# Chunked RWKV attention and a two-matmul channel mix on one core: r, k, v loaded as fp32 on SyncE's queue, matmul pieces taken from a queue, centring on ScalarE and the inverse root on GpSimd

## The chip, the core and the metric

The program runs on one core of one Trainium2 chip. A core has five engines with a queue of instructions each, executed in order: TensorE (PE, with its weight loads listed apart as PEld), VectorE (DVE), ScalarE (ACT), GpSimd (POOL) and SyncE (SP). Engines wait for each other by semaphores. Transfers from and to the memory outside the core are issued by SP, ACT or POOL and run on 16 DMA engines. The metric is the time of one execution in microseconds (us) on the device.

## What is computed

The inputs r, k and v have the shape 4 x 8 x 768 x 48 (batch, heads, time, head size), w and u 8 x 48. The first half is a linear attention with a decaying state, the second a layer norm and a channel mix with a residual:

```python
for t in range(S):
    cur = u * kt outer vt
    y[t] = rt @ (state + cur)
    state = w * state + kt outer vt
x = y as (B, S, 384)
xn = (x - mean) / sqrt(var + 1e-6) * g_ln
out = x + max(xn @ w_ch1, 0) @ w_ch2        # 384 -> 1536 -> 384
```

## The kernel before

Time is cut into chunks of 128 steps, so there are 24 tiles (4 batches of 6 chunks), each with time on the 128 partitions and 8 x 48 = 384 columns. A setup computes the powers of w (tile `T`), transposes them to the factor tile `F2`, and builds `mask`, `WLZ` and `uwI`.

For tile i the attention half runs as four pieces of code:

- `scale(i)`: r and k, packed in `rk`, are multiplied by `F2` into one of three buffers `sc`, one VectorE instruction (line 180).
- `transposes(i)`: eight TensorE transposes of `sc` into the PSUM tile `tr` (line 188), copied to `trs` by ScalarE (line 190); VectorE multiplies the two halves to `q` (line 192).
- `scores(i)`: eight matmuls into `at` (line 203), and the state and the bonus term into `s` (lines 215, 225, 235). VectorE masks `at` into `A` (two instructions, line 246) and makes the next state `Z` (line 260); ScalarE copies the bonus `cc` (line 253), GpSimd makes `Vb` from it (line 255).
- `values(i)`: matmuls into `y` (lines 276, 288); VectorE adds `Vb` to give `x` (line 298), then the statistics `stats` and `mv` (lines 302, 306) and the centred `xn` (line 308). For every second tile ScalarE takes a square root and VectorE a reciprocal: `rs` (lines 314, 315).

The channel mix works on groups of two tiles (256 columns). `ln_transposes(i)` transposes `xn` (line 327, into the same PSUM tile `tr`; copy on ScalarE, line 328). `up(g, m)` is one of six pieces of a group: six matmuls of 256 columns into `hp` (line 337) and a ReLU on ScalarE into `hT` (line 344). `down(i, m)` is one of three pieces of a tile: four matmuls of 384 columns into `o` (line 355). There is one PSUM buffer for `o`. After the third piece VectorE scales it and adds `x` (`ot`, line 364), and SP stores `ot`. `g_ln` is folded into the weights `w1_sb` in the setup, by ScalarE (line 172).

The order on every engine is the order of the code. The loop at line 396 runs over steps s: attention of tile s, three up pieces of the group of tile s - 3, three down pieces of tile s - 5, placed by hand:

```python
        up_slot(s, 0); down_slot(s, 0)
        scores(s);     scale(s + 1)
        up_slot(s, 1); ln_transposes(s - 1)
        down_slot(s, 1); values(s)
        up_slot(s, 2); down_slot(s, 2)
```

with `transposes(s)` and the load of tile s + 3 ahead of it (the lines are shortened here). Loads of r, k and v are issued by GpSimd and change fp32 to bf16 on the way; a load reads 128 x 8 pieces of 192 bytes. They stand in GpSimd's queue behind `Vb` (line 255) of the step before.

## Time and profile before

| | |
|---|---|
| time, median of 3 runs | 182.71 us (181.68 to 182.91) |
| time of the profiled execution | 183.27 us |
| its span, first to last instruction | 181.2 us |
| PE busy | 148.7 us (82%), 1646 matmuls |
| DVE busy | 125.7 us (69%) |
| ACT busy | 87.3 us (48%) |
| POOL busy | 85.9 us (47%), with the issuing of its DMAs |

Busy time is the time in which an engine executes something; matmuls are pipelined, so that their start-to-start distance, and not their length, says how dense TensorE is. The span is cut into stages below, since the first quarter, the middle and the end have different limits. "Idle before" in brackets is the time in which the engine had nothing to do before an instruction, with what ended it. Queue q0 in the DMA views holds what GpSimd issues, q1 what SP and ACT issue.

### The profile page before, as it was taken

The page shows a single profiled execution, that of the slowest core. Times are in us where ns is not written, and L with a number is a line of the kernel's source. Part 1 is how long each engine was busy: PE and PEld are TensorE (multiplying, and loading weights), DVE is VectorE, ACT ScalarE, POOL GpSimd, SP SyncE. Part 2 cuts the span into 40 slices and gives each one's busy share as a digit, 9 for nine tenths or more (in the row PEclk, how much of TensorE's full clock was granted, in tenths as well). Part 3 has the DMA queues.
Part 4 walks back from the last instruction along what each step waited for, and adds up shares of the span by engine and source line. Part 5 has one row for each costly group of instructions (what it writes and reads, how often), then busy time and mean ns, then how long its engine had stood idle before and what let it go on. Part 6 is the DMA issues. An engine that isn't in the chain of part 4 may idle for free.

```text
span 181.2 us, 4089 instructions
## 1 busy us (share of the span) xinstructions
PE 148.7 (82%) x1646; PEld 110.1 (61%) x1646; DVE 125.7 (69%) x278; ACT 87.3 (48%) x162; POOL 85.9 (47%) x105
## 2 busy tenths in 40 slices
PE   0323558969998999999989999999899999989871
PEld 0212347757676677667666866776677767767640
DVE  0843989876798797878888877878797879621211
ACT  2085262465545453654546455637455555454300
POOL 7946776754773475357536733764471101100000
PEclk9999999988999999999999999999999999999999
DMA  5999999999889968998999799699967110111121
GB/s 21 244 340 141 184 175 79 63 67 65 43 83 97 96 48 79 109 52 84 89 109 56 75 89 111 37 87 99 93 51 77 47 45 0 47 43 45 43 90 43
DMA packets 81971, 15.61 MB, mean 86 GB/s; under 512 B 76960, under 2 KB 81568, under 8 KB 81952
## 3 DMA queue, kind: packets, MB, share of 16 engines
q0 software_dynamic: 76432, 8.26, 80.0%
q1 hardware_dynamic: 5520, 7.09, 11.2%
q8 instruction: 13, 0.21, 0.5%
q14 instruction: 6, 0.05, 0.1%
HBM read 18.88 MB, written 4.72 MB: 130 GB/s over the span
## 4 chain that ended last, share of the span: by engine, by line
PE 47%; DVE 33%; issue 8%; DMA 5%; ACT 4%; SPq 2%; DVEq 0%
PE o L355 20%; PE hp L337 11%; DVE ot L364 8%; DVE stats L302 7%; DVE x L298 7%; DMA w_f<-in_moe_w_ch_dram 5%; PE at L203 5%; DVE xn L308 3%; DVE A L246 3%; DVE mv L306 2%; DVE Z L260 2%; ACT trs L190 2%; PE y L288 2%; PE s L215 2%; PE tr L327 2%
## 5 line engine op out<-in xcount | busy, mean ns | idle before, releaser
L355 PE MATMUL o<-w_sb,hT 128*128 128x384 bf16 x288 | 57.8, 325 | 8.0 <-DVE ot L364 7.7
L337 PE MATMUL hp<-xT,w_sb 128*128 128x256 bf16 x432 | 60.5, 277 | 0.0
L344 ACT ACTIVATE hT<-hp 128x512 bf16<-128x512 f32 x72 | 42.8, 597 | 25.4 <-PE hp L337 25.4
L255 POOL TENSOR_TENSOR Vb<-vv,cc 128x384 bf16<-128x384 bf16 x24 | 19.8, 826 | 66.5 <-ACT cc L253 66.5
L337 PEld LDWEIGHTS <-w_sb 128*128 128x128 bf16 x432 | 38.8, 99 | 5.1
L355 PEld LDWEIGHTS <-hT 128*128 128x128 bf16 x288 | 27.2, 97 | 23.0 <-issue 12.2
L246 DVE TENSOR_TENSOR A<-at,mask 128x512 bf16<-128x512 f32 x48 | 30.9, 685 | 9.5 <-PE at L203 9.2
L190 ACT COPY trs<-tr 128x1024 bf16<-128x1024 bf16 x24 | 24.2, 1006 | 9.1 <-PE tr L188 9.1
L364 DVE SCALAR_TENSOR_TENSOR ot<-o,rs,x 128x384 f32<-128x384 f32 x24 | 14.4, 602 | 15.1 <-PE o L355 15.1
L71 POOL DMA_DIRECT2D rk<-in_k_dram x24 | 22.6, 944 | 0.8 <-POOLq L432 0.8
L72 POOL DMA_DIRECT2D rk<-in_r_dram x24 | 21.3, 889 | 3.0 <-DMA vv<-in_v_dram 3.0
L73 POOL DMA_DIRECT2D vv<-in_v_dram x24 | 21.8, 907 | 0.0
L192 DVE TENSOR_TENSOR q<-trs 128x512 bf16<-128x512 bf16 x24 | 10.2, 425 | 14.9 <-ACT trs L190 14.8
L188 PE MATMUL tr<-ident,sc 128*128 128x128 bf16 x192 | 16.5, 236 | 4.1 <-DVE sc L180 4.1
L188 PEld LDWEIGHTS <-sc 128*128 128x128 bf16 x192 | 13.8, 106 | 7.6 <-DVE sc L180 5.1
L203 PE MATMUL at<-trs 48*128 48x128 bf16 x192 | 10.2, 229 | 8.5 <-ACT trs L190 8.5
L298 DVE TENSOR_TENSOR x<-y,Vb 128x384 f32<-128x384 f32 x24 | 13.3, 554 | 5.1 <-PE y L288 5.1
L203 PEld LDWEIGHTS <-trs 48*128 48x128 bf16 x192 | 5.8, 98 | 15.9 <-ACT trs L190 13.1
L308 DVE TENSOR_SCALAR xn<-x,mv 128x384 bf16<-128x384 f32 x24 | 14.1, 586 | 0.9
L253 ACT COPY cc<-s 128x8 f32<-128x8 f32 x24 | 4.0, 166 | 21.9 <-PE s L235 21.9
L302 DVE BATCH_NORM_STATS2 stats<-x 128x6 f32<-128x384 f32 x24 | 13.5, 560 | 0.8
L180 DVE TENSOR_TENSOR sc<-rk,F 128x768 bf16<-128x768 bf16 x24 | 13.4, 558 | 0.0
(49 smaller groups left out, 127.5 us busy)
## 6 DMA issues: line engine op xcount, KB each, us to landing
out_dram<-ot SPq DMA_DIRECT2D x24, 192.0 KB, 2.6
rk<-in_k_dram POOLq DMA_DIRECT2D x24, 96.0 KB, 3.3
rk<-in_r_dram POOLq DMA_DIRECT2D x24, 96.0 KB, 4.0
vv<-in_v_dram POOLq DMA_DIRECT2D x24, 96.0 KB, 3.9
w_f<-in_moe_w_ch_dram SPq DMA_DIRECT2D x3, 768.0 KB, 7.5
w_sb<-in_moe_w_ch_dram POOLq DMA_DIRECT2D x1, 1152.0 KB, 10.0
w_p<-in_w_dram SPq DMA_DIRECT2D x2, 0.8 KB, 2.0
u_p<-in_u_dram SPq DMA_DIRECT2D x2, 0.8 KB, 3.1
```

Of the source, the lines that this page charges most:

```text
L71: nc.gpsimd.dma_start(out=rk[:, 1], in_=k[b, :, s0 : s0 + L, :].rearrange("h t d -> t h d"))
L73: nc.gpsimd.dma_start(out=vv[:], in_=v[b, :, s0 : s0 + L, :].rearrange("h t d -> t h d"))
L188: nc.tensor.transpose(out=tp[:, j, :], in_=sc[:, j, :], identity=ident[:])
L190: nc.scalar.copy(out=tr[:], in_=tp[:].rearrange("p (a q) t -> p a q t", a=2))
L203: nc.tensor.matmul(out=at[:, par, p, :], lhsT=tr[p0 : p0 + D, 1, p, :], rhs=tr[p0 : p0 + D, 0, p, :], start=True, stop=True,)
L246: nc.vector.tensor_tensor(out=A[:, par], in0=at[:, par], in1=mask[:].unsqueeze(1).to_broadcast([P, HP, P]), op=ALU.mult,)
L298: nc.vector.tensor_tensor(out=x[:], in0=y[:, :C], in1=cc_t[i][:].rearrange("p h d -> p (h d)"), op=ALU.add)
L302: nc.vector.bn_stats(out=stats[:], in_=x[:])
L337: nc.tensor.matmul(out=hp[:, f, :], lhsT=w1_sb[:, kc, fk * P : (fk + 1) * P], rhs=xT_t[g][:, kc, :], start=(kc == 0), stop=(kc == CK - 1),)
L344: nc.scalar.activation(out=hT_t[g][:, 2 * m : 2 * m + 2, :], in_=hp[:], func=ACT.Relu)
L355: nc.tensor.matmul(out=o[:, :C], lhsT=hT_t[g][:, fk, j * P : (j + 1) * P], rhs=w2_sb[:, fk, :], start=(fk == 0), stop=(fk == FK - 1),)
L364: nc.vector.scalar_tensor_tensor(out=ot[:], in0=o[:, :C], scalar=mv_t[g][:, j : j + 1], in1=x_t[i][:], op0=ALU.mult, op1=ALU.add,)
```

## The change

It has these parts:

- r, k and v are loaded as fp32, without a change of type, by SP (k of tile 0 by ACT). SP's queue holds the loads of tiles 0 and 1, then the weights `w1_f`, now in three pieces of 512 columns, then tiles 2 and 3, and in step s the load of tile s + 4. The small loads of w, u and g move to ACT's queue.
- `F2` is fp32. VectorE scales k alone, GpSimd scales r and makes a bf16 copy `vv` of v. `Vb` is fp32.
- The weights are scaled by -g in pieces in step 1, a third each on ScalarE, VectorE and GpSimd. The sign makes up for a centring that gives mean - x.
- Centring (`xn`) is a ScalarE instruction in the step after (`center`); the inverse root is an add and a power on GpSimd. There is no square root on ScalarE and no reciprocal.
- `transposes(s + 1)` stands in step s, between the second and third group of matmuls.
- Up and down pieces go to two queues when their inputs are in the program; `fill(2)`, three times in a step, takes two of them, up and down in turn. The first piece of a tile's down is not taken in the same `fill` as the last of the tile before. Downs may begin in step 4.
- The setup's chain `wl`, `uwI`, `WLZ` runs on GpSimd; `hT` has 5 buffers, `x` 14, the loads 7.

```diff
-        rk = ld.tile([P, 2, H, D], BF16, name="rk")
-        nc.gpsimd.dma_start(out=rk[:, 1], in_=k[b, :, s0 : s0 + L, :].rearrange("h t d -> t h d"))
-        nc.gpsimd.dma_start(out=rk[:, 0], ...)
-        nc.gpsimd.dma_start(out=vv[:], ...)
+        rk = ld.tile([P, 2, H, D], FP32, name="rk")
+        vf = ld.tile([P, H, D], FP32, name="vf")
+        (k_eng or nc.sync).dma_start(out=rk[:, 1], in_=k[b, :, s0 : s0 + L, :].rearrange("h t d -> t h d"))
+        nc.sync.dma_start(out=rk[:, 0], ...)
+        nc.sync.dma_start(out=vf[:], ...)
...
     def scale(i):
-        nc.vector.tensor_tensor(out=sc_bufs[i % NSC][:, :, :, :D], in0=rk_t[i][:], in1=F2[:], op=ALU.mult)
+        sc = sc_bufs[i % NSC]
+        nc.vector.tensor_tensor(out=sc[:, 1, :, :D], in0=rk_t[i][:, 1], in1=F2[:, 1], op=ALU.mult)
+        nc.gpsimd.tensor_tensor(out=sc[:, 0, :, :D], in0=rk_t[i][:, 0], in1=F2[:, 0], op=ALU.mult)
+        vv = ld.tile([P, H, D], BF16, name="vv")
+        nc.gpsimd.tensor_copy(out=vv[:], in_=vf_t[i][:])
...
+    def scale_w1(n):
+        nc.scalar.activation(out=w1_sb[:, n, 0], in_=w1_f[:, n, 0], func=ACT.Copy, scale=g_neg[:, 0:1])
+        nc.vector.tensor_scalar(out=w1_sb[:, n, 1], in0=w1_f[:, n, 1], scalar1=g_neg[:, 1:2], ...)
+        nc.gpsimd.tensor_scalar(out=w1_sb[:, n, 2], in0=w1_f[:, n, 2], scalar1=g_neg[:, 2:3], ...)
...
-        nc.vector.tensor_scalar(out=xn[:], in0=x[:], scalar1=mv[:, i % GT, 0:1], scalar2=None, op0=ALU.subtract)
-            nc.scalar.activation(out=rs[:], in_=mv[:, :, 1], func=ACT.Sqrt, bias=eps_t[:], scale=1.0)
-            nc.vector.reciprocal(out=rs[:], in_=rs[:])
+    def center(i):
+        nc.scalar.activation(out=xn[:], in_=x_t[i][:], func=ACT.Identity, bias=mv[:, j, 0:1], scale=-1.0)
+            nc.gpsimd.tensor_scalar(out=rs[:], in0=mv[:, :, 1], scalar1=1e-6, scalar2=1.0, ...)
+            nc.gpsimd.tensor_tensor(out=rs[:], in0=rs[:], in1=expo[:], op=ALU.pow)
...
+    def fill(n):
+        clock[0] += 1
+        for _ in range(n):
+            can_up = ups and ups[0][0] <= clock[0]
+            can_down = downs and downs[0][0] <= clock[0] and clock[0] >= down_from[0]
+            if can_down and downs[0][2] == 0 and last_o[0] >= clock[0]:
+                can_down = False
+            if can_up and (turn[0] == 0 or not can_down):
+                _, g, m = ups.pop(0)
+                up(g, m)
...
+    for s in range(NT):
+        if s + 1 < NT:
+            scale(s + 1)
+        scores(s)
+        if s >= 1:
+            center(s - 1)
+        if s == 1:
+            scale_w1(0)
+        if s + 4 < NT:
+            load(s + 4)
+        if s == W2_SLOT:
+            nc.gpsimd.dma_start(out=w2_sb[:], in_=w2_src)
+        fill(2)
+        if s + 1 < NT:
+            transposes(s + 1)
+        fill(2)
+        if s >= 1:
+            ln_transposes(s - 1)
+        values(s)
+        if s == 1:
+            scale_w1(1)
+            scale_w1(2)
+        fill(2)
```

Three places show what moves. The first is SP's queue from the start of the program, of the changed kernel (before it held the small loads, `w_f`, and then only the 24 stores):

```order
L77 DMA w_c<-in_w_dram 128x3x1
L72 DMA rk<-in_r_dram 128x8x48
L73 DMA vf<-in_v_dram 128x8x48
L71 DMA rk<-in_k_dram 128x8x48
L72 DMA rk<-in_r_dram 128x8x48
L73 DMA vf<-in_v_dram 128x8x48
L97 DMA w_f<-in_moe_w_ch_dram 128x3x512 x3
L71 DMA rk<-in_k_dram 128x8x48
```

The last row is the first load of tile 2: it stands behind five loads and all of the weights `w_f`.

The second is VectorE's queue in a step of the middle, from `x` of a tile to the next `x`; first before, then of the change:

```order
L298 TENSOR_TENSOR x<-y,Vb 128x384
L302 BN_STATS stats<-x 128x6
L306 BN_AGGR mv<-stats 128x2
L308 TENSOR_SCALAR xn<-x,mv 128x384
L364 SCALAR_TENSOR_TENSOR ot<-o,rs,x 128x384
L192 TENSOR_TENSOR q<-trs 128x512
L246 TENSOR_TENSOR A<-at,mask 128x512 x2
L260 TENSOR_TENSOR Z<-s,WLZ 128x384
L180 TENSOR_TENSOR sc_164<-rk,F_146 128x16x48
```

```order
L322 TENSOR_TENSOR x<-y,Vb 128x384
L326 BN_STATS stats<-x 128x6
L330 BN_AGGR mv<-stats 128x2
L405 SCALAR_TENSOR_TENSOR ot<-o,rs,x 128x384
L204 TENSOR_TENSOR sc_133<-rk,F_155 128x8x48
L270 TENSOR_TENSOR A<-at,mask 128x512 x2
L284 TENSOR_TENSOR Z<-s,WLZ 128x384
L218 TENSOR_TENSOR q<-trs 128x512
```

`xn` is gone from between `mv` and `ot`, `sc` of the next tile stands ahead of `A` instead of behind `Z`, and `q` is that of the next tile.

The third is GpSimd's queue in steps 0 and 1 of the change (before, each `Vb` was followed by three loads):

```order
L279 TENSOR_TENSOR Vb<-vf,cc 128x384
L205 TENSOR_TENSOR sc_137<-rk,F_155 128x8x48
L207 CAST vv<-vf 128x384
L279 TENSOR_TENSOR Vb<-vf,cc 128x384
L190 TENSOR_SCALAR w_sb<-w_f,g_neg 128x512
L463 DMA w_sb<-in_moe_w_ch_dram 128x12x384
L190 TENSOR_SCALAR w_sb<-w_f,g_neg 128x512 x2
```

The first `Vb` is that of tile 0, the second that of tile 1: between them stand two instructions on the data of tile 2.

## Rows read from the trace of the kernel before

**Rows 1.** The page's part 1: busy time of each engine.

```profile
PE 148.7 (82%) x1646; PEld 110.1 (61%) x1646; DVE 125.7 (69%) x278; ACT 87.3 (48%) x162; POOL 85.9 (47%) x105
```

**Rows 2.** Windows by stage: stretch, length, busy us per engine (instructions), PEclk, DMA share, GB/s.

```profile
0.00:15.34 15.34, 2.55 (x14) 1.91 (x14) 5.92 (x31) 6.71 (x5) 11.17 (x20) 1.00 1.27 195
15.34:48.77 33.43, 25.65 (x299) 20.00 (x300) 26.44 (x57) 15.91 (x32) 22.70 (x26) 0.95 1.47 100
48.77:159.13 110.36, 104.46 (x1224) 77.55 (x1223) 89.61 (x186) 58.73 (x118) 51.99 (x60) 1.00 0.86 73
159.13:177.31 18.18, 16.00 (x112) 10.61 (x110) 3.08 (x7) 6.00 (x11) 0.00 (x0) 1.00 0.16 55
177.31:181.20 3.89, 0.00 (x0) 0.00 (x0) 0.62 (x1) 0.00 (x0) 0.00 (x0) 1.00 0.14 51
```

**Rows 3.** The chain that ended last: start us, length us, what.

```profile
4.71 9.13 DMA w_f<-in_moe_w_ch_dram
13.86 1.57 ACT w_sb L172
15.44 0.91 ACT trs L190
...
48.77 0.52 DVE ot L364
```

**Rows 4.** Timeline of TensorE in one middle step: start us, length us, instruction, [idle before].

```profile
98.77 0.81 PE L355 MATMUL o<-w_sb,hT 128*128 128x384 bf16 x4 [0.35 <-DVE ot L364]
99.51 0.40 PE L203 MATMUL at<-trs 48*128 48x128 bf16 x8
...
102.13 0.81 PE L337 MATMUL hp<-xT,w_sb 128*128 128x256 bf16 x6
102.78 0.81 PE L355 MATMUL o<-w_sb,hT 128*128 128x384 bf16 x4
103.43 0.61 PE L188 MATMUL tr<-ident,sc 128*128 128x128 bf16 x8
103.88 0.82 PE L337 MATMUL hp<-xT,w_sb 128*128 128x256 bf16 x6
105.00 0.81 PE L355 MATMUL o<-w_sb,hT 128*128 128x384 bf16 x4 [0.30 <-DVE ot L364]
```

**Rows 5.** Who waited for whom: us in total, times, longest us.

```profile
PE o L355 <- DVE ot L364: 7.7, 19, 0.7
```

**Rows 6.** DMA queue q1 in the stretches 1.8:2.4, 3.7:6 and 9:12: packets, MB, share.

```profile
q1 hardware_dynamic: 357, 0.00, 30.1%
...
q1 hardware_dynamic: 819, 0.02, 36.6%
...
q1 hardware_dynamic: 206, 1.14, 97.8%
```

**Rows 7.** DMA queue q0 in the stretch 16:17: packets, MB, share.

```profile
q0 software_dynamic: 1490, 0.14, 267.2%
```

**Rows 8.** The page's DMA issues: KB each, us from issue to landing.

```profile
w_sb<-in_moe_w_ch_dram POOLq DMA_DIRECT2D x1, 1152.0 KB, 10.0
```

**Rows 9.** Instructions by line: busy us, mean ns of one, idle before.

```profile
L344 ACT ACTIVATE hT<-hp 128x512 bf16<-128x512 f32 x72 | 42.8, 597 | 25.4 <-PE hp L337 25.4
L255 POOL TENSOR_TENSOR Vb<-vv,cc 128x384 bf16<-128x384 bf16 x24 | 19.8, 826 | 66.5 <-ACT cc L253 66.5
L298 DVE TENSOR_TENSOR x<-y,Vb 128x384 f32<-128x384 f32 x24 | 13.3, 554 | 5.1 <-PE y L288 5.1
...
masks.py:197 POOL MEMSET ident_f<- 128x128 f32 x1 | 0.2, 243 | 0.0
```

**Rows 10.** The tiles' view of two VectorE instructions: duration ns, least, median, most.

```profile
L308 DVE TENSOR_SCALAR xn<-x,mv x24: 419/619/843, 20.6 to 158.7; 128x384 bf16<-128x384 f32 x24
L180 DVE TENSOR_TENSOR sc<-rk,F x24: 545/546/705, 10.6 to 150.8; 128x768 bf16<-128x768 bf16 x24
```

More of the change, by code (lines that the diff above doesn't have):

```diff
@@ L83 @@
         for par in range(2):
-            nc.sync.dma_start(
+            nc.scalar.dma_start(
                 out=dst[par * DP : par * DP + D, :],
@@ L114 @@
     )
-    load(1)
-    load(2)
-    eps_t = const.tile([P, 1], FP32, name="eps_t")
-    nc.vector.memset(eps_t[:], 1e-6)
+    ident = const.tile([P, P], BF16, name="ident")
+    nc.vector.tensor_copy(ident[:], ident_f[:])
+    expo = const.tile([P, GT], FP32, name="expo")
+    nc.vector.memset(expo[:], -0.5)
+    NSC = 3
+    sc_bufs = []
+    for i in range(NSC):
+        t_ = const.tile([P, 2, H, DP], BF16, name=f"sc{i}")
+        nc.vector.memset(t_[:, :, :, D:DP], 0.0)
+        sc_bufs.append(t_)
+    WLZ = const.tile([P, HP, E2], FP32, name="WLZ")
+    nc.vector.memset(WLZ[:], 0.0)
+    uwI = const.tile([P, HP, 2], BF16, name="uwI")
+    nc.vector.memset(uwI[:], 0.0)
     T = const.tile([P, 2 * CK, L + 1], FP32, name="T")
@@ L243, in scores @@
             first = False
+        if c < NCH - 1:
+            if c > 0:
+                nc.tensor.matmul(
+                    out=s_ps[:, : HP * E2],
+                    lhsT=ident[:],
+                    rhs=Z_t[i - 1][:].rearrange("p q e -> p (q e)"),
+                    start=False,
+                    stop=True,
+                    skip_group_check=True,
+                )
+            for p in range(HP):
+                nc.tensor.matmul(
+                    out=s_ps[:, p * E2 : (p + 1) * E2],
+                    lhsT=ksc[:, 1, p, :],
+                    rhs=v_t[i][:, 2 * p : 2 * p + 2, :],
+                    start=False,
+                    stop=True,
+                    skip_group_check=True,
+                )
         A = sb2.tile([P, 2, HP, P], BF16, name="A")
@@ L253, in scores @@
         nc.scalar.copy(out=cc[:], in_=s_ps[:, C : C + H])
-        Vb = sb2.tile([P, H, D], BF16, name="Vb")
+        Vb = sb2.tile([P, H, D], FP32, name="Vb")
         nc.gpsimd.tensor_tensor(
-            out=Vb[:], in0=v_t[i][:], in1=cc[:].unsqueeze(2).to_broadcast([P, H, D]), op=ALU.mult
+            out=Vb[:], in0=vf_t[i][:], in1=cc[:].unsqueeze(2).to_broadcast([P, H, D]), op=ALU.mult
         )
@@ L328, in ln_transposes @@
         nc.scalar.copy(out=xT_t[g][:, :, j * P : (j + 1) * P], in_=tp[:, :CK, :])
+        if j == GT - 1:
+            for m in range(NU):
+                ups.append((clock[0] + 1, g, m))
+    NU = FK // 2
+    FB = FW // P
     def up(g, m):
         if m == 0:
-            hT_t[g] = sb2.tile([P, FK, GW], BF16, name="hT")
+            hT_t[g] = sb3.tile([P, FK, GW], BF16, name="hT", bufs=5)
         hp = ps_h.tile([P, 2, GW], FP32, name="hp")
         for f in range(2):
-            fk = 2 * m + f
+            n, fb = divmod(2 * m + f, FB)
             for kc in range(CK):
@@ L344, in up @@
         nc.scalar.activation(out=hT_t[g][:, 2 * m : 2 * m + 2, :], in_=hp[:], func=ACT.Relu)
+        if m == NU - 1:
+            for j in range(GT):
+                for d in range(NM):
+                    downs.append((clock[0] + 1, g * GT + j, d))
     NM = 3
@@ L373, in down @@
             nc.sync.dma_start(out=out[b, c * L : (c + 1) * L, :], in_=ot[:])
[L376 to L417 removed]
+    clock = [0]
@@ new lines @@
+    turn = [0]
+    last_o = [-9]
+    down_from = [99]
+    ups, downs = [], []
+    def fill(n):
[8 more added lines that the diff above has]
+                up(g, m)
+                turn[0] = 1
+            elif can_down:
+                _, i, d = downs.pop(0)
+                down(i, d)
+                if d == NM - 1:
+                    last_o[0] = clock[0]
+                turn[0] = 0
+            else:
+                break
@@ L421 @@
+    center(NT - 1)
+    fill(2)
+    ln_transposes(NT - 1)
+    while ups or downs:
+        fill(2)
 _INS = ['r', 'k', 'v', 'w', 'u', 'moe_g_ln', 'moe_w_ch1', 'moe_w_ch2']
```

195 lines of the change are left out of this document (79 added, 116 removed).

## The prediction

> **What bounds the kernel now.** I read busy time first: TensorE is busy for 82% of the span, the others for 69% or less [rows 1]. An average hides the stages, so the windows come next [rows 2]. Three limits show. Up to 15.34 us TensorE has 2.55 us of work: the chain of waits runs there through the third weight load (landing at 13.84) and the scaling of the weights on ScalarE, and only behind these, at 15.4, comes the first copy `trs` of the attention [rows 3]. From there to 48.77, where tile 0's `ot` runs, attention is latency-bound and the channel mix fills up slowly. From 48.77 to 159.13 there are 18 steps of 110.36 / 18 = 6.13 us, and TensorE is nearly full. The end is a tail of channel-mix pieces.
>
> The middle decides most. In a step's timeline [rows 4] an up piece lasts 0.65 us from start to start (102.13 to 102.78), a down piece 0.65 (102.78 to 103.43). The up piece at 103.88 is followed by the next down only at 105.00: 1.12 - 0.65 = 0.47 us lost, and the down then takes 0.74 instead of 0.65 to the next matmul (98.77 to 99.51), another 0.09. The list of waits says why: the single `o` buffer is held until `ot` has run, 19 times in 24 tiles [rows 5]. `ot` itself is late because `x`, `stats`, `mv` and `xn` stand ahead of it on VectorE. Without the wait the step is 105.00 - 98.77 - 0.56 = 5.67 us. First and last chunks of a batch leave out matmuls; by the start-to-start distances this is 0.7 us in six steps, so a dense step is 5.56 us on average.
>
> **The change, part by part.** *Middle.* The queue never puts a tile's first down into the same `fill` as the last of the tile before. By the program order at least a transposition and an up piece (0.45 + 0.65) lie between them, and `xn` is gone from VectorE, so `ot` should be done. Gain: (6.13 - 5.56) x 18 = 10.3 us. In the tail 18.18 us hold 8 up and 15 down pieces and a transposition, 15.1 us dense; the last two waits remain, as nothing is left to put between (about 0.75 us each), so 1.5 is gained.
>
> *New waits on TensorE.* `ln_transposes(s - 1)` now comes two pieces after `transposes(s + 1)`, and both use the one PSUM tile `tr`, so it waits for `trs`. Two pieces and the transposition are 1.75 us, the copy about 1.0 us plus its start; it just fits if ScalarE is free, and is late by up to one ReLU of 0.6 us [rows 9] if not. Bounds 0 and 0.6 a step; I take 0.1, 2 us in all, since one ReLU per `fill` mostly ends before the transposition does.
>
> *Load on the other engines, per step of 5.56.* VectorE has 89.61 / 18 = 4.98 us [rows 2]; it loses `xn` (0.6, [rows 10]); `sc` of half the columns from fp32 costs about what `x` with as many columns costs, 0.55 [rows 9], as before. That leaves 4.4. ScalarE has 58.73 / 18 = 3.3 and gets `xn`, at most a ReLU's 0.6: 3.9. GpSimd loses its DMA issues and has `r` (as `Vb`, 0.83), the copy of v (between the 0.24 of a memset and 0.83; taken 0.45), `Vb` 0.83 and, every second step, the add and the power. No row shows a power; between 0.1 and 0.83 each by the nearest rows, it is hidden by some 3 us of idle GpSimd either way. All this is cost at nothing while TensorE covers it.
>
> *Start.* Attention no longer waits for the weights. But the loads go to q1. No run shows 192-byte pieces there; the nearest row is that of the 4-byte pieces of the small loads: 357 packets in 0.6 us, 595 per us [rows 6], while GpSimd's queue moves 1,490 per us [rows 7]. At 595 a load of 1,024 pieces takes 1.72 us. Ahead of tile 2 stand 384 pieces of `w_c`, six loads of 1,024 and 1,152 small ones (7,680, or 12.9 us from 1.8 to 14.7), then 2.36 MB of weights at 1.14 MB in 3 us [rows 6], 6.2 us, to 20.9. Tile 2's k, r and v land at 22.6, 24.4 and 26.1, tile 3's v at 31.2, tile 4's at 36.4; tile 5's k at 38.1. `vv` of tile 2 is ahead of tile 1's `Vb` on GpSimd, so step 1 ends behind 26.1, step 2 behind 31.2, step 3 behind 36.4. After that come `vv` 0.45, `Vb` 0.83, `x` to `mv` 1.3 (39.0), `sc` 0.55 and `A` 1.3 of step 4 (40.9) and `y`: TensorE is through step 4's first two fills at about 42. At 48.77 the kernel before has done one attention step (5.67 - 3.9 = 1.8) and four up pieces (2.6) more, so the point that answers to 48.77 is 46.4. `w2` on q0 runs in this stretch (10 us, [rows 8]); beside q0, q1 moved 819 packets in 2.3 us, 356 per us [rows 6], which over 8 us costs 8 x (1 - 356/595) = 3.2 us. That gives 49.6: 0.8 later than before.
>
> Later the loads need 3 x 1.72 + 0.24 (a store's 144 packets) = 5.4 us per step: hidden, but only just.
>
> *Sum.* 181.2 + 0.8 - 10.3 - 1.5 + 2.0 = 172.2 us of span. The profiled execution took 2.07 us more than its span, and is 0.56 above the median of the runs: 173.7 us.
>
> The Trainium skill (DMA: Bandwidth & Descriptors, Issuing engine by pattern) says that transfers issued by SP or ACT are generally faster than GpSimd's. The rows here speak against it for small pieces, though with 4 bytes; were it right here, the first rival below would hold.
>
> **Rivals.** *The hardware queue is quick.* If 192-byte pieces move as on q0 (1,490 per us), tile 2 is there at 1.8 + 5.2 + 6.2 + 2.1 = 15.3 and VectorE's 4.4 us set the first steps. `trs` of tile 0 starts near 11, step 4 near 31, and the point that answers to 48.77 is about 38 to 40. The sum is then 9 to 10 us less: 164. For it: the data paths were idle for two thirds of the time while the small pieces moved (30.1%), and these came as SP issued them. Against it: nothing larger was seen on q1 at such a count.
>
> *The loads become the bound (slower).* Place: SP's queue. Tile 23's k lands at 8 + 75,232 / R us, for R packets per us: 7,680 + 1,024 to tile 2, 21 tiles of 3,072 and 14 stores of 144. Some 28 us of work follow. This passes 181.2 at R = 518; at 595 it is 162 and does not bind; at the 356 seen beside q0 it would be 247. For it: the margin is 13%. Against it: q0 is idle after `w2`, and the stretch to 2.4 includes the first packets' latency, so that 595 is rather low.
>
> *VectorE or the new waits take the gain (no change).* `xn` took 419 ns at least and 843 at most [rows 10], so something holds VectorE's instructions at times. GpSimd now works on tiles for 2.1 us a step instead of 0.83. If VectorE stood still for all of it, its step would be 6.5 us, 0.4 more than the 6.13 of now: about 185. VectorE's slack is 5.56 - 4.4 = 1.2 us; from there it decides. Against it: `sc`, with two tiles read, ran 546 in the median and 705 at most, while GpSimd was as busy [rows 10]. The Trainium skill (SBUF — State Buffer, SBUF: two separate sides) calls the port that the two engines share an exclusive lock, held for a whole instruction; the spread of `xn` agrees, the small one of `sc` speaks for short waits. With half of the slack used the time is near 180.
>
> **How the numbers follow.** My forecast 0.46 (168 to 180); the quick queue 0.24 (160 to 168); the loads as the bound 0.18 (180 to 250); VectorE or waits 0.12 (178 to 188). About 1% (1.8 us) is what a measurement of this kernel can tell from no change. Faster: 0.46 and 0.24 and a little of the third, 0.73. Within 1%: the edges of the last two, 0.10. Slower: 0.17. The range 162 to 188 leaves out the far ends of the quick queue and of the bound by loads, some 0.13. The likeliest case's own time, 173.7, is the prediction.
>
> **What would show it.** Right: no wait of `o` for `ot` in the middle; steps of 5.6 to 5.8 us; in the first 40 us, `sc` or `vv` waiting for `rk` or `vf`, with q1 near 600 packets per us; `trs` of tile 0 before 13 us. Wrong: middle steps over 6 us, either with waits for loads (the queue) or with VectorE above 5.3 us busy a step (the port); or `ln_transposes` waiting for `trs` by more than 0.3 us a step. The first steps at 4.5 us apart would show the quick queue.

## The result and the profile after

The changed kernel takes 175.31 us (median; 175.12 to 175.83), the kernel before 182.3 us on the same chip: a ratio of 0.962, 95% interval 0.958 to 0.967. The prediction was 173.7 us. The profiled execution has a span of 173.4 us, where 172.2 was forecast.

Part 1 of the page of the changed kernel answers to [rows 1]: busy us, share of the span, instructions.

```profile
PE 146.9 (85%) x1646; PEld 110.4 (64%) x1646; DVE 113.9 (66%) x236; ACT 94.6 (55%) x173; POOL 74.7 (43%) x119
```

TensorE does the same work in 7.8 us less. VectorE has lost 11.8 us and ScalarE gained 7.3. GpSimd has lost 11.2 although it now works on r and v: its DMA issues are gone.

The list of waits of the changed kernel, TensorE's rows (us in total, times, longest us), answers to [rows 5]:

```profile
PE tr L214 <- POOL sc L205: 5.7, 3, 4.1
PE tr L358 <- ACT trs L216: 4.3, 3, 2.8
PE hp L374 <- ACT xT L359: 2.7, 11, 0.4
...
PE o L396 <- DVE ot L405: 0.8, 1, 0.8
```

The wait of `o` for `ot` fell from 7.7 us in 19 places to 0.8 in one, in the tail. The third row is new and has a regular count: 11 waits in 24 tiles.

To see which stage gave what, I cut both traces at the scores of tile 4 and of tile 23, which can be found in both. Of the kernel before, the two cuts in the timeline of TensorE:

```profile
38.04 0.40 PE L203 MATMUL at<-trs 48*128 48x128 bf16 x8 [1.72 <-ACT trs L190]
...
154.76 0.40 PE L203 MATMUL at<-trs 48*128 48x128 bf16 x8
```

The windows of the changed kernel, cut in the same places (its first window is cut again where `trs` of tile 0 starts); columns as in [rows 2]:

```profile
0.00:12.51 12.51, 2.55 (x14) 1.91 (x14) 4.44 (x21) 1.76 (x3) 6.03 (x22) 1.00 1.02 196
12.51:38.53 26.02, 17.26 (x189) 13.23 (x190) 18.10 (x34) 13.05 (x23) 14.85 (x20) 1.00 1.24 212
38.53:149.80 111.27, 108.22 (x1293) 82.00 (x1290) 85.26 (x170) 71.24 (x133) 52.13 (x75) 1.00 0.58 121
149.80:173.40 23.60, 18.90 (x157) 13.23 (x156) 6.10 (x11) 8.57 (x17) 1.71 (x3) 1.00 0.14 51
```

| stretch | before | after | measured | work moved between stretches | measured at equal work | predicted |
|---|---|---|---|---|---|---|
| start to tile 4's scores | 38.04 | 38.53 | +0.5 | 36 up matmuls done instead of 24: 1.3 us | -0.8 | +0.8 |
| tile 4's to tile 23's scores | 116.72 | 111.27 | -5.4 | 12 up fewer, 8 down more: equal | -5.4 | -8.3 (18 steps) |
| from there to the end | 26.44 | 23.60 | -2.8 | 8 down fewer: 1.3 us | -1.5 | -1.5 |

(Two up pieces of 0.65 us are 12 matmuls, two down pieces of 0.65 us are 8. The prediction cut at 48.77 and 159.13, so its last columns answer to these stretches and are not the same ones.) The sum, -7.8 us, is 1.2 us short of the -9.0 forecast. The middle is 2.9 us short, and the start gave 1.6 more than I had put down.

About 1 us of the -7.8 is not the change's. In its profiled execution the kernel before had a granted clock of 0.50, the level of 1.2 GHz, for 3.4 us of the middle stretch; the third number from the end shows it (columns as in [rows 2]):

```profile
39.03:42.44 3.41, 3.41 (x31) 2.80 (x29) 2.90 (x7) 1.23 (x4) 3.15 (x4) 0.50 0.63 37
```

Executions of that kernel with a mean granted clock of 1.00 have spans of 179.7 to 180.6 us, this one has 181.2.

**The middle.** A step now takes 111.27 / 19 = 5.86 us, against 116.72 / 19 = 6.14 before and 5.66 forecast. Over the six steps of one batch, from the scores of tile 12 to those of tile 18, both kernels repeat themselves and neither has a fall of the clock: 37.07 us before, 35.19 after, 0.31 us a step less. Within a batch, steps of 5.77 and 6.13 us alternate. Of the changed kernel, the timeline in a long one:

```profile
65.24 0.33 PE L358 MATMUL tr<-ident,xn 128*128 128x128 bf16 x3
...
65.57 0.36 PE L312 MATMUL y<-vv,A 128*128 128x48 bf16 x8
65.60 0.48 ACT L359 COPY xT<-tr 128x384 bf16<-128x384 bf16 x1 [0.41 <-PE tr L358]
...
66.13 0.81 PE L374 MATMUL hp<-xT,w_sb 128*128 128x256 bf16 x6 [0.20 <-ACT xT L359]
...
66.78 0.81 PE L396 MATMUL o<-w_sb,hT 128*128 128x384 bf16 x4
...
67.53 0.17 PEld L229 LDWEIGHTS <-trs 48*128 48x128 bf16 x5 [0.32 <-issue]
```

When the second tile of a group is transposed, the group's up pieces enter the queue, and the `fill` right behind `values` takes one. Between the transposition (65.24) and that piece only the `y` matmuls stand, 0.4 us by start-to-start, while the copy `xT` lasts 0.48 us and starts late by its hand-over. So the up piece starts at 66.13 instead of 65.77: 0.36 us lost, in every second step. The last row shows a second thing: from the down piece to the next scores 0.75 us pass (66.78 to 67.53), though nothing waited for `ot`.

**The start.** `trs` of tile 0 starts at 12.51, before at 15.44 [rows 3]. But the scores of tile 4 start at 38.53, half a microsecond later than before. The chain of waits of the changed kernel shows where the lead of 2.9 us went (start us, us, what):

```profile
20.81 0.47 DVE Z L284
21.27 0.09 DVE g_neg L181
21.36 0.02 issue
21.38 0.72 ACT w_sb L184
22.10 0.91 ACT trs L216
...
25.65 2.10 DVE w_sb L187 x2
27.75 0.48 DVE sc L204
```

The weight pieces (`w_sb`) stand in the attention's way twice: `trs` of tile 2 is queued on ScalarE behind a piece that waits for `g_neg`, which VectorE makes only behind `A` and `Z` of tile 1; and two pieces on VectorE take 2.1 us ahead of `sc` of tile 3. Of the changed kernel, VectorE and GpSimd there:

```profile
21.38 0.49 DVE L187 TENSOR_SCALAR w_sb<-w_f,g_neg 128x512 bf16<-128x512 f32 x1
...
25.04 0.98 POOL L205 TENSOR_TENSOR sc<-rk,F 128x384 bf16<-128x384 f32 x1
25.57 2.19 DVE L187 TENSOR_SCALAR w_sb<-w_f,g_neg 128x512 bf16<-128x512 f32 x2
25.98 0.69 POOL L207 CAST vv<-vf 128x384 bf16<-128x384 f32 x1
26.64 0.82 POOL L279 TENSOR_TENSOR Vb<-vf,cc 128x384 f32<-128x384 f32 x1
```

One piece took 0.49 us at 21.38, where it started ahead of GpSimd's piece (21.45); these two, beside three GpSimd instructions without a break, take 0.75 and 1.52, and each ends 0.3 us behind one of GpSimd's. So some 1.2 of the 2.1 us are VectorE standing still beside GpSimd. `sc` of tile 2, higher up in the same chain, took 1.32 instead of 0.55 us beside GpSimd's scaling of r. No load of r, k or v is in this chain, though GpSimd waited 2.4 us for r of tile 2, until 18.20.

### The profile page after: what moved, and what is told of

Read it like the earlier page. It is cut to its first block, busy times and chain, and to the rows that moved or that the text cites. A ratio compares the mean times of both kernels' runs of the same rounds, so it can differ in the third digit from the quotient of the medians.

```text
span 173.4 us, 4126 instructions
## 1 busy us (share of the span) xinstructions
PE 146.9 (85%) x1646; PEld 110.4 (64%) x1646; DVE 113.9 (66%) x236; ACT 94.6 (55%) x173; POOL 74.7 (43%) x119
## 4 chain that ended last, share of the span: by engine, by line
PE 76%; DVE 10%; ACT 8%; issue 2%; DMA 1%; POOL 1%; DVEq 0%; ACTq 0%
PE hp L374 27%; PE o L396 25%; PE tr L214 7%; PE at L229 4%; ACT xT L359 3%; ACT trs L216 3%; PE tr L358 3%; PE s L240 2%; PE s L260 2%; PE y L312 2%; DMA w_c<-in_w_dram 1%; PE s L251 1%; PE y L300 1%; DVE ot L405 1%; DVE stats L326 1%
## 5 line engine op out<-in xcount | busy, mean ns | idle before, releaser
L374 PE MATMUL hp<-xT,w_sb 128*128 128x256 bf16 x432 | 58.0, 276 | 2.7 <-ACT xT L359 2.7
L396 PE MATMUL o<-w_sb,hT 128*128 128x384 bf16 x288 | 56.3, 326 | 0.9 <-DVE ot L405 0.8
L381 ACT ACTIVATE hT<-hp 128x512 bf16<-128x512 f32 x72 | 42.9, 598 | 22.6 <-PE hp L374 22.1
L279 POOL TENSOR_TENSOR Vb<-vf,cc 128x384 f32<-128x384 f32 x24 | 20.2, 841 | 66.2 <-ACT cc L277 66.2
L374 PEld LDWEIGHTS <-w_sb 128*128 128x128 bf16 x432 | 40.3, 99 | 9.0 <-issue 3.8
L396 PEld LDWEIGHTS <-hT 128*128 128x128 bf16 x288 | 27.6, 98 | 13.6 <-issue 1.4
L218 DVE TENSOR_TENSOR q<-trs 128x512 bf16<-128x512 bf16 x24 | 12.3, 512 | 25.2 <-ACT trs L216 25.1
L205 POOL TENSOR_TENSOR sc<-rk,F 128x384 bf16<-128x384 f32 x24 | 23.9, 997 | 2.4 <-DMA rk<-in_r_dram 2.4
L214 PEld LDWEIGHTS <-sc 128*128 128x128 bf16 x192 | 13.6, 105 | 10.2 <-POOL sc L205 6.5
L337 ACT ACTIVATE xn<-x,mv 128x384 bf16<-128x384 f32 x24 | 14.8, 617 | 0.7 <-DVE mv L330 0.7
L359 ACT COPY xT<-tr 128x384 bf16<-128x384 bf16 x24 | 11.5, 480 | 5.5 <-PE tr L358 5.5
L204 DVE TENSOR_TENSOR sc<-rk,F 128x384 bf16<-128x384 f32 x24 | 14.4, 599 | 0.0
L207 POOL CAST vv<-vf 128x384 bf16<-128x384 f32 x24 | 14.3, 595 | 0.0
L358 PE MATMUL tr<-ident,xn 128*128 128x128 bf16 x72 | 8.2, 225 | 4.3 <-ACT trs L216 4.3
```

The costliest lines, as they stand in the source:

```text
L205: nc.gpsimd.tensor_tensor(out=sc[:, 0, :, :D], in0=rk_t[i][:, 0], in1=F2[:, 0], op=ALU.mult)
L214: nc.tensor.transpose(out=tp[:, j, :], in_=sc[:, j, :], identity=ident[:])
L279: nc.gpsimd.tensor_tensor(out=Vb[:], in0=vf_t[i][:], in1=cc[:].unsqueeze(2).to_broadcast([P, H, D]), op=ALU.mult)
L359: nc.scalar.copy(out=xT_t[g][:, :, j * P : (j + 1) * P], in_=tp[:, :CK, :])
L374: nc.tensor.matmul(out=hp[:, f, :], lhsT=w1_sb[:, n, kc, fb * P : (fb + 1) * P], rhs=xT_t[g][:, kc, :], start=(kc == 0), stop=(kc == CK - 1),)
L381: nc.scalar.activation(out=hT_t[g][:, 2 * m : 2 * m + 2, :], in_=hp[:], func=ACT.Relu)
```

## The experiments

The changed kernel and all twelve runs at a glance; the ratio is to the kernel before, the last column the start of tile 4's scores and the step from tile 4 to 23 in the profiled execution.

| run | us | ratio (95%) | tile 4's scores, step |
|---|---|---|---|
| changed kernel | 175.3 | 0.962 (0.958 to 0.967) | 38.5, 5.86 |
| e1 without the rule | 193.5 | 1.062 (1.057 to 1.066) | 38.7, 6.82 |
| e2 centring on VectorE | 176.5 | 0.967 (0.963 to 0.972) | 38.5, 5.87 |
| e3 loads twice | 191.7 | 1.051 (1.047 to 1.055) | 38.0, 6.72 |
| e4 ups later | 172.8 | 0.947 (0.942 to 0.951) | 39.1, 5.65 |
| e5 weights scaled elsewhere | 172.4 | 0.944 (0.939 to 0.948) | 36.1, 5.86 |
| e6 loads by GpSimd | 178.9 | 0.978 (0.973 to 0.983) | 40.3, 5.96 |
| e7 r of tile 0 on VectorE | 174.3 | 0.953 (0.949 to 0.957) | 37.5, 5.86 |
| e8 weights first | 177.8 | 0.975 (0.968 to 0.981) | 41.3, 5.86 |
| e9 three edits together | 169.1 | 0.925 (0.920 to 0.930) | 35.7, 5.64 |
| e10 and q from PSUM | 170.3 | 0.933 (0.928 to 0.938) | 36.0, 5.66 |
| e11 and tile 2's loads first | 168.6 | 0.923 (0.919 to 0.928) | 34.1, 5.67 |
| e12 e9 and scaling sooner | 170.5 | 0.934 (0.930 to 0.937) | 35.7, 5.72 |

No run takes back the earlier place of `transposes(s + 1)`, the power on GpSimd or the fp32 type of the loads by itself, so what each of these is worth is not shown.

### The rule of the queue

```diff
-            if can_down and downs[0][2] == 0 and last_o[0] >= clock[0]:
-                can_down = False
```

> The changed kernel, but a tile's first down piece may again stand in the same fill as the last down piece of the tile before. My theory: the rule is what removed the waits of the `o` tile, since `ot` alone needs about 0.75 us from the last matmul to the release and nothing then stands between. Such neighbours come about every second tile, so some 11 waits of 0.4 to 0.7 us return: 4 to 7 us slower than the changed kernel (175.3), so 179 to 182, with "PE o <- DVE ot" again at 5 us or more in the list of waits. Rival (it was `xn` on VectorE that made `ot` late): the waits stay below 2 us and the time within 1 us of 175.3.

193.5 us: 18 us slower than the changed kernel, where I expected 4 to 7. The waits are as many as forecast, but three times as long. Of this run, TensorE's row in the list of waits:

```profile
PE o L396 <- DVE ot L405: 16.8, 11, 1.6
```

And the timeline around one of them:

```profile
94.77 0.61 PE L214 MATMUL tr<-ident,sc 128*128 128x128 bf16 x8
...
95.21 0.81 PE L396 MATMUL o<-w_sb,hT 128*128 128x384 bf16 x4
95.41 1.01 ACT L216 COPY trs<-tr 128x1024 bf16<-128x1024 bf16 x1 [1.01 <-PE tr L214]
...
96.46 0.62 DVE L218 TENSOR_TENSOR q<-trs 128x512 bf16<-128x512 bf16 x1 [1.26 <-ACT trs L216]
...
97.00 0.60 DVE L405 SCALAR_TENSOR_TENSOR ot<-o,rs,x 128x384 f32<-128x384 f32 x1
...
97.66 0.81 PE L396 MATMUL o<-w_sb,hT 128*128 128x384 bf16 x4 [1.64 <-DVE ot L405]
```

The last down piece of a tile now follows the transpositions (94.77) in the program. On VectorE `ot` therefore stands behind `q`, which waits for the copy `trs` of 1.01 us. `o` has been ready since about 96.0, `ot` starts at 97.00. So the rule is more than the removal of the waits of 0.4 us in [rows 5]: in the new order of the pieces a tile's `ot` is later than it was, and without the rule the change would have been a loss of 6%.

### Centring back on VectorE

```diff
         nc.vector.bn_aggr(out=mv_t[g][:, j, :], in_=stats[:])
+        xn = sb3.tile([P, C], BF16, name="xn")
+        nc.vector.tensor_scalar(out=xn[:], in0=x[:], scalar1=-1.0, scalar2=mv_t[g][:, j, 0:1], ...)
     def center(i):
-        nc.scalar.activation(out=xn[:], in_=x_t[i][:], func=ACT.Identity, bias=mv[:, j, 0:1], scale=-1.0)
```

> The changed kernel, but the centring `xn` is back on VectorE, right behind the mean, and off ScalarE; the rule of the queue stays. My theory: with the rule, `ot` has an up piece and a transposition to run in, and VectorE has slack (about 4.4 us busy of 5.86 a step, 5.0 with `xn`), so the time stays within 1.5 us of 175.3. ScalarE has 0.6 us a step less. Rival 1 (moving `xn` is part of what removed the waits of `o`): these return with 3 us or more and the time is 178 to 181. Rival 2 (ScalarE's copies are the limit behind the waits for xT and trs): the wait for xT shrinks and the time is 173 to 174.

176.5 us, the step unchanged (5.87), the waits of `o` unchanged (0.8 us, once), the waits for `xT` too. The two intervals overlap, so that the difference of 1.2 us (0.7%) can't be called a loss; the profiled spans differ by 0.3 us (173.7 and 173.4). With the rule in place, moving `xn` gave nothing that can be measured here: VectorE had room. Neither rival holds.

### The loads, twice

```diff
+        if i >= 4:
+            rk2 = ld.tile([P, 2, H, D], FP32, name="rk2")
+            vf2 = ld.tile([P, H, D], FP32, name="vf2")
+            nc.sync.dma_start(out=rk2[:, 1], in_=k[b, :, s0 : s0 + L, :].rearrange("h t d -> t h d"))
+            nc.sync.dma_start(out=rk2[:, 0], in_=r[b, :, s0 : s0 + L, :].rearrange("h t d -> t h d"))
+            nc.sync.dma_start(out=vf2[:], in_=v[b, :, s0 : s0 + L, :].rearrange("h t d -> t h d"))
```

> The changed kernel, but every load of r, k and v of the tiles from 4 on is issued twice, the second time into tiles that nothing reads. By the rate that the trace of the changed kernel shows when SP is backed up (about 1.0 us a load of 1,024 pieces) a step then needs 6 x 1.0 + 0.2 = 6.2 us, against 5.86 now: the loads just bind, 177 to 185 us, with waits for rk or vf in the middle. By the rate that I predicted with (1.72 us a load, hidden but only just) a step would need 10.5 us: 250 us or more. If the queue has far more room than that, the time stays at 175 to 176.

191.7 us: the loads bind, and harder than the 177 to 185 expected. A step takes 6.72 us. Of this run, queue q1 from 60 to 160 us (packets, MB, share of 16 engines):

```profile
q1 hardware_dynamic: 92536, 20.03, 112.4%
```

The list of waits of this run, GpSimd's longest (us in total, times, longest us):

```profile
POOL sc L211 <- DMA rk<-in_r_dram: 55.6, 16, 5.6
```

925 packets per us is the mean with stores between the loads, and 6 x 1,024 + 144 = 6,288 packets divided by it is 6.8 us, near the step measured. SP also stands waiting for `ot` in this run (21.8 us in seven places), with the loads behind the store in its queue, so that 925 is what this order reaches and the queue itself may do more. My 1.0 us a load came from a stretch of loads alone. The changed kernel needs 3,216 packets per step of 5.86 us, 549 per us: 59% of that. The prediction's 595 per us was an underestimate by a third, and its "hidden, but only just" wrong.

### Up pieces one fill later

```diff
-                ups.append((clock[0] + 1, g, m))
+                ups.append((clock[0] + 2, g, m))
```

> The changed kernel, but the up pieces of a group come ready one fill later, so that the fill right behind values holds down pieces in every step. My theory: the first up piece waits there for the copy of xT, about 0.36 us every second step (11 times); a down piece in its place takes the wait away: 3 to 4.5 us faster than 175.3, so 171 to 172.5. Rival (another wait takes its place: `o` waits again, or the up pieces run short later and TensorE waits at the end): 174.5 to 177.

172.8 us, 2.5 us faster; I had expected 3 to 4.5. No piece waits for `xT` any more, and the six steps from tile 12 to 18 take 33.95 us instead of 35.19, 0.21 a step, as the theory says. The whole middle takes 107.44 us instead of 111.27, 3.8 less, but 1.3 of these are an up and a down piece that moved into the tail. Of this run, the timeline of TensorE at the place shown above:

```profile
65.18 0.33 PE L358 MATMUL tr<-ident,xn 128*128 128x128 bf16 x3 [0.48 <-ACT trs L216]
...
65.51 0.36 PE L312 MATMUL y<-vv,A 128*128 128x48 bf16 x8
65.72 1.46 PE L396 MATMUL o<-w_sb,hT 128*128 128x384 bf16 x8
67.11 0.40 PE L229 MATMUL at<-trs 48*128 48x128 bf16 x8
```

Two down pieces follow the `y` matmuls without a gap. In the first row stands the wait that I had forecast, of the transposition for `trs`; it comes twice in this middle (0.9 us), and `o` waits for `ot` twice (0.9 us), all before 66 us. Outside, tile 4's scores start at 39.1 instead of 38.5, since the first up pieces had filled idle time, and the tail takes 24.7 instead of 23.6 us for its two more pieces. The step is 5.65 us; I had forecast 5.66 for the whole middle, new waits included.

### The weights, elsewhere and first

```diff
             center(s - 1)
         if s == 1:
-            scale_w1(0)
+            w1_act(1, 0)
+            w1_act(1, 1)
...
         values(s)
+        if s == 0:
+            w1_act(0, 0)
+            w1_act(0, 1)
+            w1_pool(0, 2)
+            w1_pool(1, 2)
         if s == 1:
-            scale_w1(1)
-            scale_w1(2)
+            w1_act(2, 0)
+            w1_act(2, 1)
+            w1_pool(2, 2)
```

`w1_act(n, kc)` scales one piece on ScalarE, `w1_pool(n, kc)` one on GpSimd; `g_neg` is made in the set-up.

> The changed kernel, but the channel-mix weights are scaled in other places: the negated g is made once in the set-up, VectorE scales nothing, ScalarE takes six pieces (behind tile 0's values, behind xn of tile 0, behind tile 1's values) and GpSimd three. My theory of the start: the long steps 1 and 2 (7.4 and 9.6 us from one tile's scores to the next's) are long because the copy trs of tile 2 stands behind a weight piece that waits 2.4 us for VectorE, and because two weight pieces of 2.2 us on VectorE stand ahead of sc of tile 3. Then tile 3's scores start 3 to 5 us before 33.7 us, and the time is 2.5 to 5 us below 175.3: 170.3 to 172.8. Rival (the loads of k, r, v set the first steps, as I predicted): the scores of tile 3 start within 1.5 us of 33.7, with waits for rk or vf in their place, and the time is 174 to 176.

172.4 us, 2.9 faster, so the start was held up by instructions. But tile 3's scores start at 31.3, 2.4 us earlier and not 3 to 5: `q` of tile 2 took 2.2 us there (below). The opposite edit puts all nine pieces ahead of tile 0:

```diff
-        if s == 1:
-            scale_w1(0)
...
+    for n in range(NW):
+        scale_w1(n)
     scale(0)
     transposes(0)
```

> The changed kernel, but all nine weight pieces are scaled in the set-up, ahead of tile 0's scaling and transpositions, as the kernel before did; everything else stays. My theory: trs of tile 0 falls back by 3 to 5.5 us from 12.5, since the last weights land near 15, but steps 1 and 2 lose the weight pieces in their chain (1.7 and 2.1 us): 175.5 to 178.5, so that moving the weights behind the attention gave 3 us at most. Rival 1 (it gave all that trs of tile 0 moved): 178.5 to 181. Rival 2 (what is late at the start is caught up by the loads' timing anyway): 174.5 to 175.5.

177.8 us. Tile 0's scores start at 20.7 instead of 13.6, 7.2 us later and not 3 to 5.5, yet the time is only 2.5 longer: steps 0 to 3 take 20.6 us instead of 25.0. Moving the weights behind the attention was worth 2.5 us, because they were put where the attention waited for them again.

### Loads of the later tiles by GpSimd

```diff
+        ld_eng = nc.gpsimd if i >= 4 else nc.sync
-        nc.sync.dma_start(out=rk[:, 0], ...)
-        nc.sync.dma_start(out=vf[:], ...)
+        ld_eng.dma_start(out=rk[:, 0], ...)
+        ld_eng.dma_start(out=vf[:], ...)
```

> The changed kernel, but the loads of r, k and v of the tiles from 4 on are issued by GpSimd again, still as fp32. My theory: an issue held GpSimd some 0.9 us each in the kernel before, so GpSimd's step goes from 2.8 to 5.5 us of 5.86: just below TensorE, but `Vb` and `sc` come later at times. 176 to 180. Rival 1 (GpSimd is covered by TensorE, so that the queue of the loads is worth nothing in the middle): 174.5 to 176. Rival 2 (the first loads of this queue and w2 stand one behind the other on it, instead of side by side, and the start gains): 172 to 174.

178.9 us, 3.6 slower, in the band. The windows of this run, 45 to 140 us:

```profile
45.00:140.00 95.00, 91.60 (x1101) 69.78 (x1099) 75.39 (x142) 60.55 (x113) 89.53 (x114) 1.00 0.52 134
```

GpSimd is busy for 94% of the middle, its issues of 0.9 us among it, and still the middle loses 1.9 us only, all of it ahead of tile 8: from there on each step is as long as in the changed kernel, as rival 1 has it. 1.8 us are lost at the start, where issues stand ahead of the scaling of r. Of the 1.9 us, 1.5 fall between tiles 7 and 8:

```profile
58.50 3.07 DVE L205 TENSOR_TENSOR sc<-rk,F 128x384 bf16<-128x384 f32 x1
...
61.63 0.40 PE L215 MATMUL tr<-ident,sc 128*128 128x128 bf16 x4 [1.31 <-DVE sc L205]
```

`sc` of k on VectorE lasts 3.07 instead of 0.55 us, while GpSimd runs its own scaling, `vv`, `Vb` and an issue without a break (58.38 to 61.49). The Trainium skill (DMA: Bandwidth & Descriptors, Issuing engine by pattern) calls transfers issued by SP or ACT generally faster; here a load lands a median 3.5 to 4.2 us after its issue on GpSimd's queue and 3.4 to 4.2 us on SP's in the changed kernel, so that this case does not show it. What SP's issue gains is GpSimd's time, and that only up to tile 8.

### r of tile 0

```diff
+        r_eng = nc.vector if i == 0 else nc.gpsimd
-        nc.gpsimd.tensor_tensor(out=sc[:, 0, :, :D], ...)
+        r_eng.tensor_tensor(out=sc[:, 0, :, :D], ...)
```

> The changed kernel, but r of tile 0 alone is scaled on VectorE, right behind k, and not on GpSimd behind wl, uwI and WLZ. The chain of waits runs there through GpSimd from 9.1 to 11.4 us. My theory: trs of tile 0 starts 1.5 to 1.8 us earlier than 12.5, and so do the scores of tiles 0 and 1; what is left of it at the end is 1 to 1.8 us (173.5 to 174.3) if the chain of instructions sets the first steps. Rival (from tile 2 on the loads set the time): the scores of tile 2 still start near 24.1 us and the time is 175 to 176.

174.3 us, 1.0 faster. Tile 0's scores start 1.9 us earlier (11.7), tile 2's 1.6 earlier (22.5), tile 4's 1.1 earlier; so that half of the lead is gone by then. The rival falls: the loads did not set the pace yet.

### Three edits together, and what binds then

The edits of e5 and e7 and this form of e4's in one kernel:

```diff
-                ups.append((clock[0] + 1, g, m))
+                ups.append((clock[0] + (2 if g else 1), g, m))
```

> The changed kernel with three edits of the earlier runs together: the up pieces come ready one fill later (here from the second group on, since the first group of them fills idle time), the channel-mix weights scaled in the other places, and r of tile 0 scaled on VectorE. One by one they gave 2.5, 2.9 and 1.0 us. My theory: the first is in the middle, the others are in two pieces of the chain at the start, so they add up: 168 to 169.8. Rival (with the instructions out of the way the loads of tiles 2 to 5 set the first steps, so that the two at the start do not add): 169.8 to 171.5, with waits for rk or vf before 40 us.

169.1 us, as the sum of the three would have it (175.3 - 6.4 = 168.9). But the chain of waits now begins, as the rival says, with a load: r of tile 2, issued at 10.1 and landed at 19.3 behind the weights. The next run sends these loads ahead of the weights (its weight pieces, one step later, are left out here):

```diff
     load(1)
+    load(2)
     for n in range(NW): nc.sync.dma_start(out=w1_f[:, n], in_=w1_src[:, n])
...
-    load(2)
     load(3)
...
```

> The kernel with the three edits together, and tile 2's loads of k, r and v issued ahead of the three weight loads instead of behind them; the weight pieces of ScalarE and GpSimd stand one step later, so that nothing of the attention stands behind a weight that has not landed. In the trace of the three edits together, the chain of waits at the start is the load of tile 2's r (issued at 10.1, landed at 19.3), which stands in the queue behind 2.36 MB of weights. My theory (the load sets the first steps now): r of tile 2 lands before 15 us, tile 2's scores start 2 to 5 us before 23.6, and 0.5 to 2 us are left of it at the end, since tile 3's loads still stand behind the weights: 167 to 168.6. Rival (the load of tile 3, or the weights that land later, take all of it): 168.7 to 170.5.

168.6 us, in the band, but its interval overlaps with that of e9, so that I can't call it faster. Tile 2's scores start at 20.0, 3.6 us sooner than in e9; tile 4's 1.7 sooner. Of this run, the chain of waits:

```profile
18.78 0.72 SPq L71
...
19.54 10.95 DMA rk<-in_r_dram
...
30.62 1.00 POOL sc L202
```

A load of r (tile 4's, for which GpSimd waits 5.8 us) takes 10.95 us from its issue, beside w2, and ahead of it the chain holds only SP's issues and one load, back to 1.8 us. The start is bound by transfers now.

The last edit starts from e9 too and moves the scaling, from the head of a step to a place ahead of `values`:

```diff
+    scale(1)
     for s in range(NT):
...
-        if s + 1 < NT:
-            scale(s + 1)
         scores(s)
...
+        if s + 2 < NT:
+            scale(s + 2)
         values(s)
```

> The kernel with the three edits together, and the scaling of tile s + 2 issued ahead of tile s's values instead of at the head of the next step, so that `sc` stands ahead of `x`, `stats` and `mv` on VectorE and the scaling of r ahead of nothing that is late on GpSimd. In the trace of the three edits together `sc` of tile 3 runs at 25.1, behind these three, though k of tile 3 is there by 23. My theory: the transpositions of tile 3 start about 1 us sooner and 0.5 to 1 us is left of it: 168 to 168.7; the middle stays at 5.65 us a step. Rival (`x` now waits behind a `sc` that waits for its load, or `Vb` behind the scaling of r): 169 to 171, with `sc` waiting for rk on VectorE or GpSimd.

170.5 us, in the rival's band; its interval just touches that of e9. Tile 3's scores start 0.8 us sooner than in e9, but tile 4's do not, `x` of tile 3 stands behind `q` and a `sc` until 36.9 instead of 35.9, and a later `ot` is late by 1.1 us. So `x` does wait behind `sc`, but not because that waits for its load: `q` lasts 1.13 us there and `sc` 0.85, where 0.42 and 0.55 are usual.

### Why q took 2.2 us

In e5 `q` of tile 2 took 2.20 us, where 0.42 is its usual time. `q` reads two operands in SBUF; the run e10 is e9 with one of them read from PSUM instead:

```diff
+        if 1 <= i <= 3:
+            nc.vector.tensor_tensor(out=q[:], in0=tp[:, :HP, :], in1=tr[:, 1], op=ALU.mult)
```

> The kernel with the three edits together, and one more: for tiles 1 to 3, q reads its first factor from the PSUM tile of the transpositions instead of from its copy in SBUF, so that this VectorE instruction reads SBUF with one operand. It tests why q of tile 2 took 2.2 us instead of 0.42 where the weights are scaled elsewhere: it started beside a GpSimd issue, weight piece and scaling of r and ended only where the last of them had ended. My theory (two SBUF operands wait for GpSimd's instructions, one does not): q of tiles 1 to 3 takes 0.4 to 0.65 us each, and 0.5 to 1.8 us fall away: 167 to 168.8, or that much below the three edits. Rival (q was only waiting for something else, such as trs or the memory): q of tile 2 stays above 1.2 us and the time is within 0.4 us of the three edits.

Of e9, the timeline of VectorE and GpSimd at tile 3 (start us, length us, instruction):

```profile
27.34 1.28 DVE L215 TENSOR_TENSOR q<-trs 128x512 bf16<-128x512 bf16 x1
27.35 0.98 POOL L202 TENSOR_TENSOR sc<-rk,F 128x384 bf16<-128x384 f32 x1
```

Of e10, at the same place:

```profile
27.11 0.42 DVE L216 TENSOR_TENSOR q<-tr,trs 128x512 bf16<-128x512 bf16 x1
27.12 0.98 POOL L202 TENSOR_TENSOR sc<-rk,F 128x384 bf16<-128x384 f32 x1
```

The same pair, 0.01 us apart: with two SBUF operands `q` lasts 1.28 us and ends 0.3 us after GpSimd's instruction, with one it lasts 0.42. So `q` did wait for GpSimd, in e9 and at this place. The time did not fall (170.3 us): in e9 the long `q` was not in the chain, and reading `tr` holds that tile, so that the transposition of `xn` waits for `q` (3.1 us in two places). The size of the effect is shown, the gain of 0.5 to 1.8 us was a miss.

## Why the prediction was right and where it was wrong

**The wait of `o`: right.** I read 0.47 us lost per step from distances in one step of the timeline. Where nothing else comes between (e4, tiles 12 to 18), a step fell from 37.07 / 6 = 6.18 to 33.95 / 6 = 5.66: 0.52. Of the two reasons that I gave, the rule was needed (e1), the move of `xn` was not (e2). The tail's 1.5 us came out at equal work.

**The 0.09 us behind the wait: wrong.** I put the 0.74 us from the down piece to the scores in [rows 4] down to the wait in front of that piece. After the change there is no wait, and it is still 0.75 (66.78 to 67.53 above). The loss belongs to the scores, whatever stands ahead of them: in both kernels 258 ns pass from the last matmul of a down piece to their first, 162 to 168 to the first of any other group, and in e1, where an up piece stands there seven times between 50 and 145 us, 205 instead of 109. This is 0.1 us a step, 1.8 in the sum. The dense step is 5.66 us, not 5.56.

**The new wait: right in kind, wrong in place.** I expected the transposition of `xn` to wait for `trs`, 0.1 us a step. In the middle it does so once, in its first step (0.45 us); with two more ahead of it that makes 4.3 us. The wait that came is one instruction further: the up piece behind the copy `xT`, 0.36 us every second step, 11 times, some 4 us in all; e4 shows it by taking it away. I had followed the moved transposition back to what it waits for, and not forward to who waits for it. That the rule of the queue lets a piece run in the `fill` right behind was in the code. This is the step that failed: the 0.1 us a step were put to the wrong instruction, and the one that waits costs 0.2. With the 0.09 it explains the middle: 5.66 + 0.2 = 5.86.

**The other engines: right in the middle.** Per step of the middle VectorE has 85.26 / 19 = 4.5 us (4.4 forecast), ScalarE 3.75 (3.9), GpSimd 2.7 (2.3). The scaling of r takes 1.0 us (0.83 forecast), the copy of v 0.6 (0.45), the power 0.71, in its bounds. None of them sets the middle.

**The start: nearly the right size, by a wrong mechanism.** I had tile 2's loads landing at 22.6 to 26.1 and the first four steps waiting for them. GpSimd starts to scale r of tile 2 at 18.2, just as it lands and after a wait of 2.4 us, but the chain holds no load of r, k or v. Of the changed kernel, queue q1 in 16:20, and SP's issues of loads (start us, us):

```profile
q1 hardware_dynamic: 4137, 0.78, 136.8%
```

```profile
17.68 0.99 SPq L73 DMA_DIRECT2D vf<-in_v_dram  x1
18.71 1.00 SPq L71 DMA_DIRECT2D rk<-in_k_dram  x1
...
25.06 4.87 SPq L71 DMA_DIRECT2D rk<-in_k_dram  x1
```

1,034 packets per us, one load of 1,024 pieces a microsecond. My 595 came from a stretch of 0.6 us in which the first small pieces were moved, and I had noted that it was rather low without taking a higher value. Beside `w2`, on the other hand, the queue moved 167 packets per us (below), not my 356. The gain that the faster queue offered was lost to the weight pieces and to r of tile 0 on GpSimd (e5, e7), costs that I had put at nothing without a reason: that attention no longer waits for the weights was said, but not where they went. Two errors of opposite sign met. That the start came out within 1.6 us of the forecast, and with it the sum, is luck. Of my signs of being right, the wait of `o` and `trs` of tile 0 before 13 us came; the step (5.86, not 5.6 to 5.8) and q1 near 600 did not.

**The rivals.** The loads as the bound fell in the changed kernel: 549 of some 925 packets per us. It is true of the start once the instructions are out of the way (e11). The quick queue was half right: 1,034, not 1,490, and its 164 us would have needed a start that the instructions could use; the best kernel here reaches 168.6. VectorE standing still for GpSimd exists and is measurable, but it costs the changed kernel's middle nothing: `q` has grown from 425 to 512 ns in the mean over 24 tiles, 2.1 us in all, beside VectorE's slack of 1.4 us a step. At the start it does cost, some 2 us of the chain (`sc` of tile 2 and the weight pieces, above), and in e6 once in the middle. My price for it was wrong besides: a step 0.4 us longer than 6.13 is 7 us in 18 steps, which gives about 189 by my own terms and not 185.

## What to carry over

When a wait is removed by reordering, follow the moved instruction in both directions: what it waits for, and who waits behind it, and also what is queued ahead of the instruction that will release it (e1: `ot` behind `q`). Work moved off a chain must be costed where it lands: weights moved behind the attention gave 2.5 of 7.2 us, and 2.9 more as soon as they stood where an engine was idle. A queue's rate is not to be read from a stretch as short as my 0.6 us, in which no transfer had landed yet: loads here take 3 to 4 us from issue to landing.
